# Attention with a gated output on one core: the opening stage recorded by the planner's clocked loop instead of a hand-written order

## The chip, the cores and the metric

The kernel runs on one core of a Trainium2 chip. The metric is the device time of one execution in microseconds (us). Three runs of the kernel before gave a median of 683.1 us (683.1 to 683.62).

## What is computed

```python
xn = layernorm(x)                       # x: 2048 tokens x 512
q = xn @ wq                             # 32 heads of 16
k = xn @ wk; v = xn @ wv                # one head of 16, shared by all
p = softmax(q k^T / 4)                  # 2048 x 2048 for each head
s = (p v) @ wo
g = silu(silu(xn @ w1) @ w2)            # 512 -> 1792 -> 512
out = x + s * g
```

## The kernel before

**Blocks.** The 32 heads by 2048 queries make 32 groups, each of four heads by 512 queries. A group runs over 16 key tiles of 128. One group and one key tile are a tile (512 in all), and one head of it is a block of 128 keys by 512 queries (2048 in all). TensorE computes a block's scores with one matmul (line 577). The exponential goes one of two ways. The first, called A, is ScalarE's exponential over two blocks at once, 128x1024, out of the two PSUM tiles psA (`exp_A`, line 606). The second, called D, is VectorE: `exp_D` (line 628) writes 16-bit integers whose bits are a rough exponential, and GpSimd adds two shifted copies of a whole tile (line 639). A tile of D thus has three versions, weighted to a better exponential, and costs three products with v where a tile of A costs one. D takes its scores from the banks D, D1 (the two halves of psD) and F (psF). The products with v gather in psO by fours (`emit_PV`, line 676). D's versions are kept in four slots: three of `ph_sb` and one made of the part of `x_sb` that holds the first 12 token tiles. A tile's slot is its running number modulo 4.

**The rest of the work.** The layer norm goes by quarters of 512 tokens, each of four token tiles. VectorE takes statistics (line 338) and aggregates them (341), GpSimd makes the reciprocal root by a power (345, 347), VectorE computes the bias -mean times rstd (359) and normalises (369). TensorE transposes (377), VectorE copies out (389), and TensorE and VectorE make k (412, 424) and v (438, 445). k is then copied by four small DMAs on SyncE's queue to a second layout for odd groups (430). Later there are dense jobs in bank F, called q, h, z and w (844), with a tanh on ScalarE for h and z (882).

**What sets the order.** `Sched` keeps a model clock for each engine and turns each recorded operation into an instruction with its semaphore waits. After the opening, one loop (from line 1111) asks the model when TensorE is free and when ScalarE needs its next scores, gives the time between to dense jobs and products with v in slots of 0.2163 us, and picks VectorE's next task among those that are ready (`advance_v`). The opening is not recorded by this loop. It is a list by hand: the first quarter (lines 467 to 489), then 12 key tiles of the first group, all on A (`NFRONT`, lines 1084 to 1108), with the layer norm's VectorE work at given tiles (`dve_pre`, 505), the TensorE work of the later quarters at given halves of tiles (`pe_pre`, 534), and matmuls on zeros (`warm`, 329) where there was nothing else. Banks are fixed there: transposes in psD, the halves of k in F and D1, v in D.

Of the kernel before, what the change touches and what calls it, by code (L numbers as in the profile page):

```python
# [13 lines left out]
P = 128  # L14
DH = 16
NQ = 512
# [180 lines left out]
def bass_recurrent_scan__grouped_kv_mqa__dense_activation_silu__prompt_kernel(  # L197
# [33 lines left out]
    AGE2 = 12.0  # L231
    KEEP, ENDQ, ROUND, MAXJOB, AHEAD, Q_EARLY = 0.6, 12, 3.0, 2, 3, 0.20
    LEAD, LEAD_END, SLIP, AGE, AGE1, MARGIN = 3, 3, 0.15, 2.0, 1.2, 0.0
    NF, F_FROM, F_LEFT, F_LATE, DENSE_END, HOLD, F_BEHIND = 14, 0.05, 9, 3, 0.95, 10, 0

    with ExitStack() as es:
# [32 lines left out]
        nb_sb = sb("nb_sb", [P, NT], FP32)  # L269
# [23 lines left out]
        def load_x(a, b, queue="sp"):  # L293
            op(queue, lambda e: e.dma_start(x_sb[:, a:b, :], xv[:, a:b, :]), writes=[("x", t) for t in range(a, b)],
               lane=f"lx{a}", cost=2.0 if b - a == 1 else 5.0)
# [5 lines left out]
        op("sp", lambda e: e.dma_start(wkn_sb[:], A_wk.rearrange("(dc p) e -> p dc e", p=P)), writes=["wkn"], lane="lwk")  # L301
        load_x(4, 8)
        op("sp", lambda e: e.dma_start(wq_sb[:], A_wq.rearrange("(dc p) n -> p dc n", p=P)), writes=["wq"], lane="lwq", cost=8.0)
        op("sp", lambda e: e.dma_start(wv_sb[:], A_wv.rearrange("(dc p) e -> p dc e", p=P)), writes=["wv"], lane="lwv")
# [6 lines left out]
        op("gp", lambda e: e.memset(mhalf_sb[:], -0.5), writes=["mhalf"])  # L311
        op("gp", lambda e: e.memset(scr_i[:], 0), writes=["scri"])
        op("v", lambda e: e.memset(zero_sb[:], 0.0), writes=["zero"])

# [22 lines left out]
        def stats(t):  # L337
            op("v", lambda e: e.bn_stats(stats_sb[:, t, :], x_sb[:, t, :]), reads=[("x", t)], writes=[("st", t)])  # L338

        def aggr(t):  # L340
            op("v", lambda e: e.bn_aggr(mv_sb[:, t, :], stats_sb[:, t, :]), reads=[("st", t)], writes=[("mv", t)])
# [8 lines left out]
        def rstd_sqrt(c):  # L350
            sl = slice(4 * c, 4 * c + 4)
            op("v", lambda e: e.tensor_scalar(rstd_sb[:, sl], mv_sb[:, sl, 1], LN_EPS, None, op0=ALU.add),
               reads=[("mv", t) for t in tiles(c)], writes=[("rstd", c)])
            op("a", lambda e: e.activation(rstd_sb[:, sl], rstd_sb[:, sl], ACT.Sqrt), reads=[("rstd", c)], writes=[("rstd", c)])
            op("v", lambda e: e.reciprocal(rstd_sb[:, sl], rstd_sb[:, sl]), reads=[("rstd", c)], writes=[("rstd", c)])

        def nbias(c):
            sl = slice(4 * c, 4 * c + 4)
            op("v", lambda e: e.scalar_tensor_tensor(out=nb_sb[:, sl], in0=mv_sb[:, sl, 0], scalar=-1.0, in1=rstd_sb[:, sl],
                                                     op0=ALU.mult, op1=ALU.mult),  # L360
               reads=[("mv", t) for t in tiles(c)] + [("rstd", c)], writes=[("nb", c)])

        def normalise(t, eng):
            rd = [("x", t), ("rstd", t // 4), ("nb", t // 4)]
            if eng == "a":
                op("a", lambda e: e.activation(xn_sb[:, t % 8, :], x_sb[:, t, :], ACT.Identity, bias=nb_sb[:, t:t + 1],
                                               scale=rstd_sb[:, t:t + 1]), reads=rd, writes=[("xn", t % 8)])
            else:
                op(eng, lambda e: e.tensor_scalar(xn_sb[:, t % 8, :], x_sb[:, t, :], rstd_sb[:, t:t + 1], nb_sb[:, t:t + 1],  # L369
                                                  op0=ALU.mult, op1=ALU.add), reads=rd, writes=[("xn", t % 8)])  # L370

        psT = psD[:, :].bitcast(BF16)

        def transposes(t):
            def f(e):
                for dc in range(NDC):
                    r = e.transpose(psT[:, (t % 4) * NQ + dc * P:(t % 4) * NQ + (dc + 1) * P], xn_sb[:, t % 8, dc * P:(dc + 1) * P],  # L377
                                    ident[:, :])
                return r
            op("pe", f, reads=[("xn", t % 8), "ident"], writes=["D1" if t % 4 > 1 else "D"])  # L380

        def evac_T(c, half, eng):
            src = psT[:, 2 * half * NQ:(2 * half + 2) * NQ].rearrange("p (t dc q) -> p t dc q", t=2, dc=NDC)
            dst = xnT_sb[:, :, c * NQ + 2 * half * P:c * NQ + (2 * half + 2) * P].rearrange("p dc (t q) -> p t dc q", t=2)
            rd, wr = ["D1" if half else "D"], [("xnT", c, half)]
            if eng == "a":
                op("a", lambda e: e.activation(dst, src, ACT.Copy), reads=rd, writes=wr)
            else:
                op("v", lambda e: e.tensor_copy(dst, src), reads=rd, writes=wr)

        def first_T(t, bank, key, eng):
# [7 lines left out]
            op("pe", f, reads=[("xn", t), "ident"], writes=[key])  # L399
# [9 lines left out]
        def mm_K(c, bank, key, a=0, b=NQ):  # L409
# [7 lines left out]
            op("pe", f, reads=rd + ["wkp"], writes=[key])  # L417

        def evac_K(c, bank, key, a, b, writes, eng="v"):
            dst, src, wr = kT_sb[0][:, c * NQ + a:c * NQ + b], bank[:, a:b], [("kT", 0, w) for w in writes]  # L420
            if eng == "a":
                op("a", lambda e: e.activation(dst, src, ACT.Copy), reads=[key], writes=wr)
            else:
                op("v", lambda e: e.tensor_copy(dst, src), reads=[key], writes=wr)  # L424
# [9 lines left out]
        def mm_V(c, bank, key):  # L434
# [6 lines left out]
            op("pe", f, reads=xnT_keys(c) + ["wv"], writes=[key])  # L441

        def evac_V(c, bank, key):
# [5 lines left out]
                reads=[key, "phw"], writes=[("v", c)])  # L449

        def mm_Q(c, t, dcs=range(NDC)):
            def f(e):
                for dc in dcs:
                    r = e.matmul(psF[:, :], lhsT=wq_sb[:, dc, t * P:(t + 1) * P], rhs=xnT_sb[:, dc, c * NQ:(c + 1) * NQ],
                                 start=(dc == 0), stop=(dc == NDC - 1))
                return r
            op("pe", f, reads=xnT_keys(c) + ["wq"], writes=["F"], cost=("full", [None] * len(dcs), NQ))

        def evac_Q(c, t, eng):
            dst = qT_sb[:, c % 2, t, :]  # L460
            if eng == "a":
                op("a", lambda e: e.activation(dst, psF[:, :], ACT.Copy, scale=QSCALE), reads=["F"], writes=[("qT", c % 2, t)])
            else:
                op("v", lambda e: e.tensor_scalar(dst, psF[:, :], QSCALE, None, op0=ALU.mult), reads=["F"], writes=[("qT", c % 2, t)],
                   cost=0.69)
# [7 lines left out]
        nbias(0)  # L473
        normalise(0, "v")
        normalise(1, "a")
        normalise(2, "v")
        normalise(3, "gp")
        first_T(0, psD[:, 0:NQ], "D", "a")
        first_T(1, psD[:, NQ:2 * NQ], "D1", "a")
        first_T(3, psA[0][:, 0:NQ], "A0", "v")  # L480
        first_T(2, psO[:, :], "O", "v")
        mm_K(0, psA[1], "A1", 0, P)
        evac_K(0, psA[1], "A1", 0, P, ["first"], "a")
        op("a", lambda e: e.activation(scr_sb[:, 0:1], rstd_sb[:, 0:1], ACT.Exp), reads=[("rstd", 0)], writes=["scr"])
        stats(4)
        warm(NWARM2, psF[:, :], "F")
        mm_Q(0, 0)
        mm_K(0, psO, "O", P, NQ)
        evac_Q(0, 0, "v")


        def ln_rest(c):
            nbias(c)
            for t in tiles(c):
                normalise(t, "v")

        def ln_aggr(c):
            for t in tiles(c):
                aggr(t)
            rstd_pow(c)  # L500

        def first_add():
            op("gp", lambda e: e.int64_add(scr_i[:, :].bitcast(I64), scr_i[:, :].bitcast(I64), 1), reads=["scri"], writes=["scri"])

        dve_pre = {
            0: [lambda: evac_K(0, psO, "O", P, NQ, [0, 1]), lambda: move_K(0), late_loads, lambda: stats(5), lambda: stats(6), lambda: stats(7),
                lambda: ln_aggr(1), lambda: evac_V(0, psD, "D"), lambda: stats(8), lambda: stats(9)],
            1: [lambda: ln_rest(1)],
            3: [lambda: stats(10), lambda: stats(11), lambda: ln_aggr(2)],
            4: [lambda: ln_rest(2)],  # L510
            5: [lambda: stats(12), lambda: stats(13)],
            7: [lambda: stats(14), lambda: stats(15), lambda: ln_aggr(3), first_add],
            8: [lambda: ln_rest(3)],
        }

        def quarter_T(c, t):
            transposes(4 * c + t)
            if t % 2:
                evac_T(c, t // 2, "v")

        def quarter_K(c):
            mm_K(c, psF, "F", 0, NQ // 2)

        def quarter_K2(c):
            mm_K(c, psD[:, NQ:2 * NQ], "D1", NQ // 2, NQ)
            evac_K(c, psF, "F", 0, NQ // 2, [2 * c])
            evac_K(c, psD[:, NQ:2 * NQ], "D1", NQ // 2, NQ, [2 * c + 1])
            move_K(c)

        def quarter_V(c):  # L530
            mm_V(c, psD, "D")
            evac_V(c, psD, "D")

        pe_pre = {}
        for c in (1, 2, 3):
            if c == 1:
                pe_pre[(1, 1)] = lambda: [quarter_T(1, 0), quarter_T(1, 1)]
                pe_pre[(2, 0)] = lambda: [quarter_T(1, 2), quarter_T(1, 3), quarter_K(1)]
            else:
# [259 lines left out]
        def next_job(t):  # L799
            if sum(h == "job" for h in hold.values()) >= MAXJOB:  # L800
                return None
# [422 lines left out]
```

## Time and profile before

| what | us |
|---|---|
| median of three runs | 683.1 |
| the profiled execution | 684.74 |
| its span (what the trace covers) | 682.9 |
| ScalarE busy | 665.0 (97%) |
| TensorE matmuls busy | 640.3 (94%) |
| VectorE busy | 589.6 (86%) |
| GpSimd busy | 369.3 (54%) |
| first exponential starts | 11.84 |
| first D copy-out starts | 37.88 |
| last exponential ends | 673.68 |

PE is TensorE, PEld its weight loads, DVE VectorE, ACT ScalarE, POOL GpSimd, SP SyncE. L606 is line 606. A row of the timeline gives start, duration, engine, line, operation, output, input, shapes, how many were merged, and in brackets the idle time before it with what ended it. The duration of a merged row runs from the first start to the last end. A row of the windows gives the stretch, then for each engine the busy time and the number of instructions, the granted TensorE clock as a share of full speed, and DMA.

### The profile page before, as it was taken

The page shows a single profiled execution, that of the slowest core. Times are in us where ns is not written, and L with a number is a line of the kernel's source. Part 1 is how long each engine was busy: PE and PEld are TensorE (multiplying, and loading weights), DVE is VectorE, ACT ScalarE, POOL GpSimd, SP SyncE. Part 2 cuts the span into 40 slices and gives each one's busy share as a digit, 9 for nine tenths or more (in the row PEclk, how much of TensorE's full clock was granted, in tenths as well). Part 3 has the DMA queues.
Part 4 walks back from the last instruction along what each step waited for, and adds up shares of the span by engine and source line. Part 5 has one row for each costly group of instructions (what it writes and reads, how often), then busy time and mean ns, then how long its engine had stood idle before and what let it go on. Part 6 is the DMA issues. An engine that isn't in the chain of part 4 may idle for free.

```text
span 682.9 us, 14794 instructions
## 1 busy us (share of the span) xinstructions
PE 640.3 (94%) x6224; PEld 185.9 (27%) x6303; DVE 589.6 (86%) x976; ACT 665.0 (97%) x759; POOL 369.3 (54%) x375
## 2 busy tenths in 40 slices
PE   8999999999999999999999999999999999999986
PEld 3432222222222222222222222222222222222222
DVE  7788888779898889988888898998898989889985
ACT  5999999999999999999999999999999999999995
POOL 5134554456565556465564565556555556756553
PEclk9999999999999999999999999999999999999999
DMA  8310000000000001000000000000000000000100
GB/s 296 119 36 1 1 2 1 1 1 2 1 1 1 2 16 32 16 3 1 1 1 2 2 1 1 17 17 16 18 1 1 1 1 2 1 2 16 48 1 32
DMA packets 10194, 12.25 MB, mean 18 GB/s; under 512 B 2000, under 2 KB 9424, under 8 KB 10128
## 3 DMA queue, kind: packets, MB, share of 16 engines
q1 hardware_dynamic: 8960, 7.25, 3.6%
q0 software_dynamic: 736, 3.67, 1.5%
q8 instruction: 49, 0.80, 0.5%
q10 hardware_dynamic: 432, 0.39, 0.2%
q14 instruction: 17, 0.14, 0.1%
HBM read 8.95 MB, written 2.10 MB: 16 GB/s over the span
## 4 chain that ended last, share of the span: by engine, by line
ACT 88%; PE 7%; DVE 3%; DMA 0%; POOL 0%; issue 0%; DVEq 0%
ACT pa_sb L606 83%; ACT t_sb L882 5%; PE psA L577 2%; PE psO L676 2%; DVE stats_sb L338 1%; PE psF L844 1%; PE psF L329 0%; DVE ph_sb L628 0%; DMA x_sb<-in_A_x_dram 0%; PE psD L377 0%; DVE xn_sb L369 0%; POOL rstd_sb L347 0%; PE psD L412 0%; PE psF L412 0%; DVE kTa_sb L424 0%
## 5 line engine op out<-in xcount | busy, mean ns | idle before, releaser
L606 ACT ACTIVATE pa_sb<-psA 128x1024 bf16<-128x1024 f32 x678 | 644.4, 1189 | 3.9 <-PE psA L577 2.0
L639 POOL INT64_ADD ph_sb<-ph_sb x260 | 268.7, 1046 | 214.6 <-DVE ph_sb L628 214.6
L628 DVE TENSOR_SCALAR ph_sb<-psD 128x512 int16<-128x512 f32 (+1 forms) x464 | 321.9, 703 | 49.8 <-PE psD L577 41.3
L676 PE MATMUL psO<-ph_sb,vaug_sb 128*32 128x512 bf16 x1560 | 204.0, 385 | 0.4 <-ACT pa_sb L606 0.2
L676 PE MATMUL psO<-pa_sb,vaug_sb 128*32 128x512 bf16 x1356 | 202.9, 385 | 0.6 <-DVE vaug_sb L445 0.3
L577 PE MATMUL psA<-qT_sb,kTa_sb 32*128 32x512 bf16 x692 | 134.2, 384 | 10.2 <-ACT pa_sb L606 7.0
L577 PE MATMUL psA<-qT_sb,kTb_sb 32*128 32x512 bf16 x664 | 129.2, 386 | 11.8 <-ACT pa_sb L606 9.8
L639 POOL INT64_ADD x_sb<-x_sb x86 | 89.0, 1047 | 63.1 <-DVE x_sb L628 63.1
L577 PE MATMUL psD<-qT_sb,kTb_sb 32*128 32x512 bf16 x327 | 120.1, 386 | 0.4 <-DVE ph_sb L628 0.4
L628 DVE TENSOR_SCALAR x_sb<-psD 128x512 int16<-128x512 f32 (+1 forms) x149 | 104.0, 702 | 15.2 <-PE psD L577 14.0
L577 PE MATMUL psD<-qT_sb,kTa_sb 32*128 32x512 bf16 x309 | 112.0, 384 | 0.0
L676 PE MATMUL psO<-x_sb,vaug_sb 128*32 128x512 bf16 x516 | 92.9, 386 | 0.1
L577 PEld LDWEIGHTS psA<-qT_sb,kTa_sb 32*128 32x128 bf16 x692 | 32.5, 91 | 141.8 <-ACT pa_sb L606 129.0
L577 PEld LDWEIGHTS psA<-qT_sb,kTb_sb 32*128 32x128 bf16 x664 | 31.2, 91 | 144.5 <-ACT pa_sb L606 132.9
L676 PEld LDWEIGHTS psO<-ph_sb,vaug_sb 128*32 128x32 bf16 x1560 | 51.7, 95 | 50.7 <-issue 33.1
L844 PE MATMUL psF<-xnT_sb,w_sb 128*128 128x512 bf16 x194 | 60.9, 384 | 3.9 <-issue 2.4
L844 PE MATMUL psF<-w_sb,u_sb 128*128 128x512 bf16 x205 | 61.3, 383 | 2.5 <-issue 1.9
L676 PEld LDWEIGHTS psO<-pa_sb,vaug_sb 128*32 128x32 bf16 x1356 | 50.8, 94 | 45.2 <-issue 30.1
L882 ACT ACTIVATE t_sb<-psF 128x512 bf16<-128x512 f32 x72 | 55.2, 766 | 0.0
L914 DVE SCALAR_TENSOR_TENSOR u_sb<-t_sb,psF 128x512 bf16<-128x512 bf16 x56 | 38.3, 683 | 8.3 <-ACT t_sb L882 7.8
L577 PEld LDWEIGHTS psD<-qT_sb,kTb_sb 32*128 32x128 bf16 x327 | 28.3, 91 | 0.9 <-DVE ph_sb L628 0.7
L676 PEld LDWEIGHTS psO<-x_sb,vaug_sb 128*32 128x32 bf16 x516 | 23.1, 95 | 16.0 <-issue 11.2
(98 smaller groups left out, 361.1 us busy)
## 6 DMA issues: line engine op xcount, KB each, us to landing
w_sb<-in_B_w_dram POOLq DMA_DIRECT2D x2, 1792.0 KB, 12.3
x_sb<-in_A_x_dram SPq DMA_DIRECT2D x18, 128.0 KB, 2.3
out_dram<-ob_sb SPq DMA_DIRECT2D x15, 128.0 KB, 1.7
x_sb<-in_A_x_dram SPq DMA_DIRECT2D x3, 512.0 KB, 6.9
wq_sb<-in_A_wq_dram SPq DMA_DIRECT2D x1, 512.0 KB, 6.4
wop_sb<-in_A_wo_dram SPq DMA_DIRECT2D x1, 512.0 KB, 10.1
x_sb<-in_A_x_dram ACTq DMA_DIRECT2D x2, 128.0 KB, 3.1
kTb_sb<-kTa_sb SPq DMA_DIRECT2D x16, 16.0 KB, 2.9
```

The lines of the kernel that those rows point to most:

```text
L338: op("v", lambda e: e.bn_stats(stats_sb[:, t, :], x_sb[:, t, :]), reads=[("x", t)], writes=[("st", t)])
L577: return e.matmul(ap, lhsT=kT_sb[g % 2][32 * i:32 * i + 32, kt * P:(kt + 1) * P], rhs=qT_sb[32 * i:32 * i + 32, c % 2, g // 2, :], start=T ...
L606: d = op("a", lambda e: e.activation(pa_sb[:, sl, :], psA[k][:, :], ACT.Exp, scale=ESCALE), reads=["A%d" % k], writes=[("pa", sl)], cost=2 ...
L628: d = op("v", lambda e: e.tensor_scalar(ph_ap(0, sl, 512 * pos, 512 * pos + m), src, float(PH_ONE + PH_BIAS), 0.0, op0=ALU.add, op1=ALU.ma ...
L639: d = op("gp", lambda e, j=j: e.int64_add(ph_ap(j, sl, 0, 2048).bitcast(I64), ph_ap(0, sl, 0, 2048).bitcast(I64), PH_SHIFT[j] * 0x00010001 ...
L676: r = e.matmul(psO[32 * i:32 * i + 32, :], lhsT=vaug_sb[:, p["v"], p["kt"], :], rhs=p["ap"], start=s0, stop=s1, tile_position=(0, 32 * i), ...
L844: h = e.matmul(ap, lhsT=l, rhs=r, start=(m == 0), stop=(m == end))
L882: op("a", lambda e: e.activation(t_sb[:, n % 2, :], bank_ap(b), ACT.Tanh, scale=0.5 if jb[0] == "h" else 0.25), reads=[b], writes=[("t", n ...
L914: op("v", lambda e: e.scalar_tensor_tensor(out=dst, in0=t_sb[:, n % 2, :], scalar=1.0, in1=src, op0=ALU.add, op1=ALU.mult), reads=tk["read ...
```

## The change

The order of the opening after the first quarter comes from the loop. Statistics, aggregation, normalisation and copies out become VectorE tasks with ranks (`st`, `ag`, `nm`, `T`, `K`, `V`). Transposes, k and v of the later quarters become front jobs, which the loop puts in whichever of D, D1 and F is free. The lists by hand and their zero matmuls go; the loop's own filler stays.

The first quarter changes too. All four first normalisations are on VectorE, as subtract the mean and multiply by rstd, so the bias instruction goes in all quarters. The root is taken by ScalarE directly from the variance with a bias of eps, and the Exp table is asked for right after it. q's first 128 columns are computed in two halves of 256 tokens, each copied out by ScalarE. Three of the second quarter's statistics stand ahead of this. The loads of wo, w1 and w2 are recorded after the second quarter's power on GpSimd's queue.

For D, a tile's slot is chosen when the tile is opened (`free_slot`), not by its running number. While k isn't complete, only one tile of the second group may go to D, and none of the first. GpSimd's shifted copies are held back until its last power has been recorded. SLIP goes from 0.15 to 0.2.

```diff
-    AGE2 = 12.0
+    AGE2, AGE_ST, FIRST, FRONT_D, FRONT_K, SHORT, ST_EARLY, Q_ACT = 12.0, 1.5, 9.4, 1, 4, 0, 3, 1
-    LEAD, LEAD_END, SLIP, AGE, AGE1, MARGIN = 3, 3, 0.15, 2.0, 1.2, 0.0
+    LEAD, LEAD_END, SLIP, AGE, AGE1, MARGIN = 3, 3, 0.2, 2.0, 1.2, 0.0
...
         def rstd_sqrt(c):
             sl = slice(4 * c, 4 * c + 4)
-            op("v", lambda e: e.tensor_scalar(rstd_sb[:, sl], mv_sb[:, sl, 1], LN_EPS, None, op0=ALU.add),
-               reads=[("mv", t) for t in tiles(c)], writes=[("rstd", c)])
-            op("a", lambda e: e.activation(rstd_sb[:, sl], rstd_sb[:, sl], ACT.Sqrt), reads=[("rstd", c)], writes=[("rstd", c)])
-            op("v", lambda e: e.reciprocal(rstd_sb[:, sl], rstd_sb[:, sl]), reads=[("rstd", c)], writes=[("rstd", c)])
+            op("a", lambda e: e.activation(rstd_sb[:, sl], mv_sb[:, sl, 1], ACT.Sqrt, bias=eps_sb[:, 0:1]),
+               reads=[("mv", t) for t in tiles(c)] + ["eps"], writes=[("rstd", c)], cost=4)
+            op("a", lambda e: e.activation(scr_sb[:, 0:1], mhalf_sb[:, 0:1], ACT.Exp), reads=["mhalf"], writes=["scr"], cost=4)
+            K.act_end += 1.28
+            op("v", lambda e: e.reciprocal(rstd_sb[:, sl], rstd_sb[:, sl]), reads=[("rstd", c)], writes=[("rstd", c)], cost=0.2)
...
         def normalise(t, eng):
+            op(eng, lambda e: e.tensor_scalar(xn_sb[:, t % 8, :], x_sb[:, t, :], mv_sb[:, t, 0:1], rstd_sb[:, t:t + 1],
+                                              op0=ALU.subtract, op1=ALU.mult),
+               reads=[("x", t), ("mv", t), ("rstd", t // 4)], writes=[("xn", t % 8)], cost=0.41)
...
-        nbias(0)
-        normalise(0, "v")
-        normalise(1, "a")
-        normalise(2, "v")
-        normalise(3, "gp")
+        for t in tiles(0):
+            normalise(t, "v")
         first_T(0, psD[:, 0:NQ], "D", "a")
         first_T(1, psD[:, NQ:2 * NQ], "D1", "a")
+        first_T(2, psO[:, :], "O", "v")
         first_T(3, psA[0][:, 0:NQ], "A0", "v")
-        first_T(2, psO[:, :], "O", "v")
         mm_K(0, psA[1], "A1", 0, P)
         evac_K(0, psA[1], "A1", 0, P, ["first"], "a")
-        op("a", lambda e: e.activation(scr_sb[:, 0:1], rstd_sb[:, 0:1], ACT.Exp), reads=[("rstd", 0)], writes=["scr"])
-        stats(4)
+        for t in range(4, 4 + ST_EARLY):
+            stats(t)
         warm(NWARM2, psF[:, :], "F")
-        mm_Q(0, 0)
+        first_Q((0, 1), psF, "F")
+        first_Q((2, 3), psD, "D")
+        first_evac_Q(0, 2, psF, "F", "a")
+        first_evac_Q(2, 4, psD, "D", "a" if Q_ACT else "v")
+        for t in range(4 + ST_EARLY, 8):
+            stats(t)
+        for t in range(4, 8):
+            aggr(t)
+        rstd_pow(1)
         mm_K(0, psO, "O", P, NQ)
-        evac_Q(0, 0, "v")
+        evac_K(0, psO, "O", P, NQ, [0, 1])
+        move_K(0)
+        late_loads()
...
+        RANK = dict(T=0, K=0, V=0, ag=2, nm=3, st=4)
...
+        for c in range(1, NC):
+            if c > 1:
+                for t in tiles(c):
+                    task("st", ln_st, 0.687, t=t, reads=[("x", t)], writes=[])
+                task("ag", ln_ag, 0.4, c=c, reads=[], writes=[], need=[("st", t) for t in tiles(c)])
+            for t in tiles(c):
+                task("nm", ln_nm, 0.41, t=t, reads=[("rstd", c)], writes=[], need=[("ag", c)] + ([("T", t - 8)] if t >= 8 else []))
...
+        front = [("V", 0)] + [jb for c in range(1, NC) for jb in (("T", c, 0), ("T", c, 1), ("K", c, 0), ("K", c, 1), ("V", c))]
...
+        def next_front(t):
+            return next((jb for jb in front[:2] if front_ready(jb, t)), None)
...
         def next_job(t):
+            if progress() < F0:
+                return None
...
+        def free_slot(gi):
+
+            used = {slot_of[o["idx"]] for o in dst["open"] + dst["fifo"]}
+            best = None
+            for sl in range(NPD):
+                if sl in used or (sl == 3 and not all(("nm", n) in tok for n in range(12))):
+                    continue
+                keys = {ph_key(j, sl, p) for j in range(NPH) for p in range(4)}
+                n = [sum(p["key"] in keys for p in q) for q in pend]
+                if any(n[gi + 1:]) or any(slot_of[a[1]] == sl for a in shifts):
+                    continue
+                if best is None or sum(n) < best[0]:
+                    best = (sum(n), sl)
+            return None if best is None else best[1]
...
         def next_D(t):
...
+                    if ("kT", 0, NKT // 2 - 1) not in tok and (gi == 0 or NKT - len(left[gi]) >= FRONT_D or ("kT", 0, FRONT_K) not in tok):
+                        continue
+                    if free_slot(gi) is None:
+                        continue
...
         def fill_D(t, free):
...
+            if front:
+                keep = max(keep, len(banks) - 1 + sum(h == "blk" for h in hold.values()))
...
-        for u in range(NFRONT):
-            for _ in range(2):
-                exp_A(*front.pop(0))
-            for f in dve_pre.get(u, []):
-                f()
...
+        K.act_end = max(K.act_end, FIRST)
+        K.free["a"] = max(K.free["a"], FIRST - 0.3)
...
+            late = more and ast["tile"] is None and not kt_ready((group_A(), left[group_A()][0]), t + (0.1 if state["n"] else 0.4))
+            blocked = blocked or late
...
+                jb = next_front(t)
+                if jb and slots >= 2:
+                    b = free_banks(t + 0.04)
+                    if b:
+                        emit_front(jb, b[0])
+                        did = 2
+                can = job_ready(t) and not did
```

`front_ready` asks the model whether a job's inputs are there; `emit_front` records its matmuls in the bank and makes the copy-out a VectorE task; `first_Q` is four matmuls of 128 columns for each token tile; `kt_ready` asks whether a key tile's k has arrived.

## Prediction

> **What bounds the kernel now.** I read the page's busy line and its costliest group first, then ScalarE's timeline from the start, the chain of waits of the opening, VectorE's timeline there, and the stretches with a granted clock under 1.
>
> ```profile
> PE 640.3 (94%) x6224; PEld 185.9 (27%) x6303; DVE 589.6 (86%) x976; ACT 665.0 (97%) x759; POOL 369.3 (54%) x375
> L606 ACT ACTIVATE pa_sb<-psA 128x1024 bf16<-128x1024 f32 x678 | 644.4, 1189 | 3.9 <-PE psA L577 2.0
> ```
>
> ScalarE is the bound. A ledger shows how closely. The chain has 24 exponentials in 22.00 us, so 0.917 us each; 72 tanh add 0.49 us each. From the first start, 677 x 0.917 = 620.8, plus the last one's 1.02, plus 72 x 0.49 = 35.3, is 657.1 us. The first exponential starts at 11.84 and the last ends at 673.68, which is 661.8 us. So ScalarE loses only 4.7 us in all. Where?
>
> ```profile
> 9.42 1.28 ACT L484 ACT_TABLE_LOAD   x1
> 10.71 0.21 ACT L484 ACTIVATE scr_sb<-rstd_sb 128x1 bf16<-128x1 f32 x1
> 11.84 2.85 ACT L606 ACTIVATE pa_sb<-psA 128x1024 bf16<-128x1024 f32 x3 [0.92 <-PE psA L577]
> 15.07 3.98 ACT L606 ACTIVATE pa_sb<-psA 128x1024 bf16<-128x1024 f32 x4 [0.37 <-PE psA L577]
> 19.38 4.01 ACT L606 ACTIVATE pa_sb<-psA 128x1024 bf16<-128x1024 f32 x4 [0.33 <-PE psA L577]
> 37.84 14.81 ACT L606 ACTIVATE pa_sb<-psA 128x1024 bf16<-128x1024 f32 x16
> ```
>
> The last row is the 26th exponential, found by narrowing the window. At 0.917 us it would start at 11.84 + 25 x 0.917 = 34.77; it starts at 37.84. **The opening loses 3.07 us**, all on TensorE. The chain shows how:
>
> ```profile
> 15.88 0.54 PE psF L329 x2
> 16.42 0.33 PE psO L676 x4
> 16.75 0.32 PE psA L577 x2
> 17.07 0.55 PE psD L377 x8
> ```
>
> Two zero matmuls, one round of products and one pair of scores take 0.54 + 0.33 + 0.32 = 1.19 us where 0.917 is to be had. A half of a quarter's transposes with scores is 0.55 + 0.32 = 0.87, which fits.
>
> The other loss is late. In 656.00 to 659.00 TensorE is about half busy; then the clock is halved:
>
> ```profile
> 658.00:659.00 1.00, 0.47 (x6) 0.15 (x3) 1.00 (x4) 1.00 (x2) 1.00 (x2) 1.00 0.00 0
> 660.00:661.00 1.00, 1.00 (x10) 0.10 (x2) 1.00 (x3) 1.00 (x2) 0.44 (x1) 0.50 0.00 0
> 662.00:663.00 1.00, 1.00 (x12) 0.25 (x12) 0.00 (x0) 0.51 (x2) 0.71 (x1) 0.50 0.00 0
> ```
>
> (The clock is the third number from the end.) Exponentials starting at 660.08, 661.45, 662.97 and 664.29 span 4.21 us instead of 2.75: 1.46 us. 3.07 + 1.46 is 4.5 of the 4.7.
>
> Between these ScalarE is full, so there the time falls only if D takes tiles from A. D begins here:
>
> ```profile
> 31.60 0.17 DVE L359 SCALAR_TENSOR_TENSOR nb_sb<-mv_sb,rstd_sb 128x4 f32<-128x4 f32 x1 [1.17 <-POOL rstd_sb L347]
> 34.98 0.69 DVE L389 COPY xnT_sb<-psD 128x1024 bf16<-128x1024 bf16 x1 [0.94 <-PE psD L377]
> 37.88 0.69 DVE L628 TENSOR_SCALAR ph_sb<-psD 128x512 int16<-128x512 f32 x1 [0.26 <-PE psD L577]
> ```
>
> VectorE waits for GpSimd's power and for TensorE's transposes, and D starts when the layer norm is through, at 37.88. ScalarE does 678 x 2 = 1356 of 2048 blocks, 2.05 per us over 661.8 us. D does the other 692 until about 665, 1.10 per us.
>
> **The first quarter.** From the aggregates' end (6.25) before has 0.17 (line 352), the root, the reciprocal and 0.16 (line 359). The two that go cost 0.17 + 0.16 and two gaps of 0.03: 0.39 us. The normalisations start at 6.74 instead of 7.13, and on VectorE alone take 0.32 to 0.42 each (four in 1.38 at line 369), ends at 7.15, 7.47, 7.79, 8.11. But the gain is covered: the table load now stands between the root (6.29 to 6.49) and the first copies out. 6.51 + 1.28 + 0.21 = 8.00, and before the first copy started at 8.04. So ScalarE's copies (1.08 for two) and k's (0.28) end at 9.36 instead of 9.40: worth 0.04.
>
> The 1.28 + 0.21 at 9.42 go, but they lay beside q's matmuls and copy. The path there is TensorE's zero matmuls until 9.52 (same in both), then q. Now each token tile is 4 matmuls of 128 columns, 0.22 us as the transposes at 8.40. Two tiles end at 9.52 + 0.44 + 0.19 (the drain: 1.04 for four of 512 against 4 x 0.213) = 10.15, the next two at 10.59. ScalarE's copy of 256 columns is bounded by its 0.28 for 128 and 1.02 for 1024; interpolated it is 0.39. The second ends at 11.02, against VectorE's 11.27 before. k's remaining matmuls (0.65) end at 11.05, beside it. With 0.03 to 0.14 to the scores and 0.43 to the exponential as before, the first starts at **11.5** (11.3 by 0.28, 11.9 if the copy costs the 0.69 of VectorE's and they queue). Worth 0.3 us. wq lands at 2.66 + 6.4 = 9.06, in time by 0.46.
>
> The Trainium skill's page "ScalarE: Activation LUTs", section "What ACT_TABLE_LOAD costs", speaks against this place for the load: it gives a switch about 2.66 us, with a drain. By it, the first copy would start 1.38 us later. The trace has 1.28 us, with the copy of k ending at 9.40 and the next instruction at 10.71, so no drain shows here. By the page's figure the saving below would be 0.9 us less (1.38 x 0.65).
>
> **Key tiles in time.** Exponentials 1 to 8 need the first quarter's k; the second quarter's must be there at 11.5 + 8 x 0.917 = 18.8, less 0.43. VectorE has three statistics after 9.03 and a fourth (0.62 each), then aggregates until 11.9, so GpSimd's power (0.24 + 1.04) ends at 13.3, not 15.35. Normalisation, transposes, copy, half of k and its copy took 15.39 to 19.55 before, 4.2 us: 17.5, in time by 0.9. The later quarters have more.
>
> **Loads and GpSimd.** w1 and w2 move from 8.07 to about 13.3 on GpSimd's queue, behind the power. They took 12.3 us and land by 29; the first tanh was at 52.45. Nothing. Ahead of GpSimd's first shifted copy lie 5.9 us of idle "issue" before line 503; it now starts when the last power ends, some 5 us earlier, and four slots cover it.
>
> **Front jobs.** 16 jobs take 0.5 to 0.6 us of TensorE each, one in a gap of scores, and products only where two more slots remain. Bounds of what ScalarE still loses: 0 and the 3.07 of before. I take 0.8, nearer to the row in which 0.87 fits into 0.917, with some products colliding. Worth 2.3.
>
> **D's start.** VectorE was busy 18.9 us from 11.84 to 36.00 and 0.8 more until 37.88: 19.7. Three biases go (0.5), two statistics move ahead (1.2): 18.0 from 11.5, so 29.5 at best. Before it idled 6.3; I leave 1.5, since statistics can now fill waits: **D from 31.0**, 6.9 us earlier. Bounds: 29.5 and 37.9.
>
> **The sum.** ScalarE is ahead by 0.3 + 2.3 = 2.6 us, D by 6.9. If the end comes s earlier, the blocks gained and given up at the end balance: 2.05 (2.6 - s) + 1.10 (6.9 - s) = 0, s = (5.3 + 7.6) / 3.15 = 4.1 us. That is about three more blocks on D, nearly one tile. The profiled execution's span 682.9 becomes 678.8 (its time 684.74 becomes 680.6; 1.6 of that lies over the median). The median 683.1 becomes **679.0**.
>
> Free slots and SLIP are charged at nothing: products and banks decide D's rate now (VectorE idles 41.3 us waiting for scores in ph_sb's rows). One tile of D more or less is two exponentials, 1.83 us.
>
> **Rivals.**
> - D's head start is lost again at the end (lead and group ends are unchanged): only 2.6 us remain, 680.5. For it: tiles come whole, and 2.8 us of net lead times 1.10 is only three blocks.
> - The clock drop at 660 doesn't recur: up to 1.46 us more, 677.6. For it: it followed one stretch at half load, and the order changes. Two tiles more on D instead: 2.6 + 3.66, 676.8.
> - The front jobs wait as before, or the clock drops in the opening, where 11 recorded zero matmuls go: one drop costs 1.46. ScalarE keeps 0.3 us and D two blocks: 682.3. Against it: filler stays, and TensorE's useful work is denser. The skill's page "TensorE: Matmul & The Clock Gate" ("What's actually happening") says that low activity over a window of about 3.4 us halves the clock; the drop at 660 agrees, after 3 us at 0.47 to 0.56 busy.
> - **Slower**: `free_slot` refuses tiles in the steady part, since a slot that owes products to a later group is shut at opening, where before only the copy-out waited. Each refused tile is 1.83 us. Beyond two it eats the 4.1; with four of 173, 683.1 - 4.1 + 7.3 = 686.3. Against it: any of four slots may now serve.
> - The order isn't what it claims (a misjudged landing stalls one queue): also under the last two.
>
> **The numbers.** Forecast 0.36; lead lost 0.20; no clock drop or more tiles 0.24; opening no better 0.10; slower 0.10. 0.2% (1.4 us) is about what a measurement here can tell from no change: faster means under 681.7. The first three cases and a little of the fourth are faster, 0.82; same 0.09; slower 0.09. The range takes in the first four: 675.5 (more tiles and no drop) to 683.0.
>
> **What would show it.** The first exponential at 11.5; the 26th by 35.3; the first steady D copy-outs near 31; some 676 exponentials; the table load at 6.5 with the first copy at 8.0. A first exponential after 12, gaps <-PE psA in the opening, or over 680 exponentials would prove me wrong.

## The result and the profile after

The changed kernel takes 687.81 us (median of 8 runs, 686.95 to 689.76). The kernel before, run beside it, takes 683.37 us (683.1 to 686.04). The ratio is 1.0061, with a 95% interval of 1.0042 to 1.008: 4.4 us slower by the medians, where 4.1 us faster was forecast. (A run that took over 1.5% longer than its kernel's fastest, one of e5's twelve and two of e8's below, is left out of the ratios but not of the medians.) The profiled execution has a span of 686.4 us (time 688.22), 3.5 us more than before.

The page of the changed kernel, busy line and costliest group:

```profile
PE 640.7 (93%) x6232; PEld 186.9 (27%) x6310; DVE 591.9 (86%) x985; ACT 664.3 (97%) x760; POOL 368.9 (54%) x373
L547 ACT ACTIVATE pa_sb<-psA 128x1024 bf16<-128x1024 f32 x678 | 642.8, 1177 | 7.2 <-PE psA L518 6.2
```

The work is the same: 678 exponentials, as before. What grew is the last figure, the idle time ahead of the exponentials: 7.2 us instead of 3.9, of which 6.2 instead of 2.0 wait for A's scores (line 518). ScalarE's timeline of the changed kernel says where they lie:

```profile
6.62 1.28 ACT L355 ACT_TABLE_LOAD   x1
8.02 1.07 ACT L392 ACTIVATE xnT_sb<-psD 128x512 bf16<-128x512 bf16 x2
10.81 0.38 ACT L454 ACTIVATE qT_sb<-psF 128x256 bf16<-128x256 f32 x1 [1.44 <-PE psF L446]
12.23 11.10 ACT L547 ACTIVATE pa_sb<-psA 128x1024 bf16<-128x1024 f32 x12 [0.56 <-PE psA L518]
23.60 3.77 ACT L547 ACTIVATE pa_sb<-psA 128x1024 bf16<-128x1024 f32 x4 [0.27 <-PE psA L518]
31.23 1.02 ACT L547 ACTIVATE pa_sb<-psA 128x1024 bf16<-128x1024 f32 x1 [3.86 <-PE psA L518]
33.17 2.11 ACT L547 ACTIVATE pa_sb<-psA 128x1024 bf16<-128x1024 f32 x2 [0.92 <-PE psA L518]
35.65 17.52 ACT L547 ACTIVATE pa_sb<-psA 128x1024 bf16<-128x1024 f32 x19 [0.37 <-PE psA L518]
```

The table load stands where the prediction put it, and the first copy starts at 8.02. The 13th exponential is at 23.60, the 20th at 35.65. Seven at 0.917 us are 6.42; they take 12.05. So **5.6 us are lost between 23.6 and 35.7**, mostly in three gaps. The 26th starts at 41.09; before it was 37.84. That is 3.25 later, and the span is 3.5 longer: nearly all of the difference between the two profiles arises before this point.

The chain of waits of the changed kernel (start, duration, what) names the cause:

```profile
18.57 10.91 DMA kTb_sb<-kTa_sb
29.52 0.60 PE psD L518
30.12 0.53 PE psF L428 x16
30.66 0.54 PE psA L518 x2
```

A small DMA lies on it: the copy of the second quarter's k to the layout for odd groups (16 KB each, line 420), issued at 18.57 and landed at 29.5. TensorE's timeline shows who waits:

```profile
25.77 0.39 PE L518 MATMUL psA<-qT_sb,kTa_sb 32*128 32x512 bf16 x2
29.52 0.60 PE L518 MATMUL psD<-qT_sb,kTb_sb 32*128 32x512 bf16 x1 [3.36 <-DMA kTb_sb<-kTa_sb]
30.06 0.60 PE L428 MATMUL psF<-wv_sb,xnT_sb 128*128 128x16 bf16 x16
30.59 0.61 PE L518 MATMUL psA<-qT_sb,kTa_sb 32*128 32x512 bf16 x2
```

This is the one early D tile that the change allows (FRONT_D = 1). It belongs to the second group, which is odd and reads kTb. Its first score stands in TensorE's queue at 26.15 and waits 3.36 us. The next scores for ScalarE, ready to run, stand behind it. After the wait the matmuls take 0.60 us instead of 0.39. The windows of the changed kernel (stretch, length, busy time of PE, PEld, DVE, ACT, POOL, granted clock, DMA share, GB/s) show why:

```profile
24.00:28.00 4.00, 2.16 (x17) 0.90 (x14) 2.64 (x5) 3.37 (x4) 0.00 (x0) 1.00 0.93 302
28.00:32.00 4.00, 2.48 (x31) 1.00 (x31) 1.28 (x6) 0.77 (x1) 0.42 (x2) 0.50 0.09 24
```

The clock is halved from 28 us on, still in the wait, until about 34. And the DMA engines are nearly full until 28: w1 and w2 (3.67 MB) now go out at 13.30 and 14.46 on GpSimd's queue, not at 8.07 and 9.14. wo (512 KB) is on SyncE's own queue, in both kernels; here it goes out at 14.99, just ahead of the copy, and lands 14.0 us later, at 29.0: half a microsecond before it.

So the theory after the result was: a late copy of k, read too early, holds TensorE, and the clock drop adds to it. Its rivals: the wait is only where another loss shows; the clock drop is the greater part; and, for the copy itself, full engines against a queue of its own that is blocked.

### The profile page after: what moved, and what is told of

Read it like the earlier page. It is cut to its first block, busy times and chain, and to the rows that moved or that the text cites. A ratio compares the mean times of both kernels' runs of the same rounds, so it can differ in the third digit from the quotient of the medians.

```text
span 686.4 us, 14802 instructions
## 1 busy us (share of the span) xinstructions
PE 640.7 (93%) x6232; PEld 186.9 (27%) x6310; DVE 591.9 (86%) x985; ACT 664.3 (97%) x760; POOL 368.9 (54%) x373
## 3 DMA queue, kind: packets, MB, share of 16 engines
q0 software_dynamic: 736, 3.67, 1.5%
## 4 chain that ended last, share of the span: by engine, by line
ACT 89%; PE 6%; DMA 3%; DVE 1%; issue 0%; SPq 0%; DVEq 0%
ACT pa_sb L547 84%; ACT t_sb L914 5%; PE psO L629 2%; PE psA L518 2%; DMA kTb_sb<-kTa_sb 2%; DMA wq_sb<-in_A_wq_dram 1%; PE psF L876 1%; PE psF L330 0%; PE psD L518 0%; DVE ph_sb L569 0%; SPq L294 0%; DVE x_sb L569 0%; PE psA L1201 0%; DVE wq_sb L1214 0%; DVE onb_sb L712 0%
## 5 line engine op out<-in xcount | busy, mean ns | idle before, releaser
L589 POOL INT64_ADD ph_sb<-ph_sb x294 | 304.3, 1048 | 233.8 <-DVE ph_sb L569 233.6
L569 DVE TENSOR_SCALAR ph_sb<-psD 128x512 int16<-128x512 f32 (+1 forms) x528 | 359.8, 691 | 54.9 <-PE psD L518 43.9
L629 PE MATMUL psO<-ph_sb,vaug_sb 128*32 128x512 bf16 x1764 | 212.9, 385 | 0.3 <-POOL ph_sb L589 0.2
L518 PE MATMUL psA<-qT_sb,kTa_sb 32*128 32x512 bf16 x692 | 134.8, 386 | 10.1 <-ACT pa_sb L547 6.9
L518 PE MATMUL psD<-qT_sb,kTa_sb 32*128 32x512 bf16 x309 | 113.4, 384 | 0.4 <-DVE ph_sb L569 0.4
L589 POOL INT64_ADD x_sb<-x_sb x52 | 53.8, 1046 | 44.6 <-DVE x_sb L569 44.6
L569 DVE TENSOR_SCALAR x_sb<-psD 128x512 int16<-128x512 f32 (+1 forms) x95 | 65.9, 699 | 12.0 <-PE psD L518 10.3
L629 PEld LDWEIGHTS psO<-ph_sb,vaug_sb 128*32 128x32 bf16 x1764 | 53.4, 95 | 56.0 <-issue 37.8
L629 PE MATMUL psO<-x_sb,vaug_sb 128*32 128x512 bf16 x312 | 54.5, 384 | 0.0
L569 DVE TENSOR_SCALAR ph_sb<-psF 128x512 int16<-128x512 f32 x51 | 34.5, 676 | 0.0
```

The costliest lines, as they stand in the source:

```text
L518: return e.matmul(ap, lhsT=kT_sb[g % 2][32 * i:32 * i + 32, kt * P:(kt + 1) * P], rhs=qT_sb[32 * i:32 * i + 32, c % 2, g // 2, :], start=T ...
L569: d = op("v", lambda e: e.tensor_scalar(ph_ap(0, sl, 512 * pos, 512 * pos + m), src, float(PH_ONE + PH_BIAS), 0.0, op0=ALU.add, op1=ALU.ma ...
L589: d = op("gp", lambda e, j=j: e.int64_add(ph_ap(j, sl, 0, 2048).bitcast(I64), ph_ap(0, sl, 0, 2048).bitcast(I64), PH_SHIFT[j] * 0x00010001 ...
L629: r = e.matmul(psO[32 * i:32 * i + 32, :], lhsT=vaug_sb[:, p["v"], p["kt"], :], rhs=p["ap"], start=s0, stop=s1, tile_position=(0, 32 * i), ...
```

## The experiments

Each kernel is the changed kernel with the edit shown. "Before" is always run on the same chip.

### Who waits: e1 and e3

```diff
-    ... = 12.0, 1.5, 9.4, 1, 4, 0, 3, 1
+    ... = 12.0, 1.5, 9.4, 0, 4, 0, 3, 1     (e1: FRONT_D = 0)
```

> The changed kernel, but no tile of the second group may go to D before all of k is there (FRONT_D 0). In the changed kernel's trace TensorE stands still from 26.15 to 29.52 at the early D tile's first scores, which read a copy of k whose DMA was issued at 18.57 and landed 10.9 us later, and the clock is 0.50 afterwards; ScalarE loses 5.6 us between 23.60 and 35.65. Theory W (this wait): the gap of 3.86 us and the halved clock go, the 26th exponential starts near 36, and the time is 682.5 to 684.5. Rival S (free_slot and SLIP make D slower in the steady part): the opening mends but the time stays over 686. Rival L (the moved loads hurt in more ways than this wait): some gap over 2 us remains in the opening, 685 to 687.

Measured: 681.79 us, ratio 0.9962 (0.9946 to 0.9979). The copy is as slow as ever (up to 11.0 us), but no one reads it early. ScalarE's timeline of e1 has 26 exponentials in a row:

```profile
23.40 23.94 ACT L547 ACTIVATE pa_sb<-psA 128x1024 bf16<-128x1024 f32 x26 [0.27 <-PE psA L518]
```

In e3 the early D tile stays, but the planner's model takes the copy for 12 us long, and so takes a key tile of the first quarter for it:

```diff
-                   writes=[...], lane=f"mk{c}{i}")
+                   writes=[...], lane=f"mk{c}{i}", cost=12.0 if c == 1 else 3.0)
```

> The changed kernel with one number of the model changed: the copy of the second quarter's k is charged 12 us instead of 3. TensorE's order stays the same by name; the early D tile takes a key tile of the first quarter, whose copy was issued at 12.5. Theory W: the wait at 26.15 goes or falls under 1 us, 682 to 684.5. If the wait were for the bank or the queue and not for this copy, nothing changes: 687.5 to 688.

Measured: 681.94 us, 0.9967 (0.9954 to 0.9981). The D score runs at 25.54 without a wait, and 26 exponentials start from 23.36 without a gap. The early tile does no harm; its reading of the late copy does. Both undo the loss and leave a gain over before.

### Which load makes the copy late: e2, e7, e13, e14

e2 issues w1 and w2 early again (8.54 and 9.62); e7 issues them late (22.02 and 23.10), behind the third quarter's power and the landing of the second quarter's copies.

```diff
 def late_loads():
     wo on SyncE's queue
-    w1, w2 on GpSimd's queue
...
 (e2: right behind the four first normalisations)
+    w1, w2 on GpSimd's queue, reads=[("xn", 3)]
 (e7: in ln_ag, behind the third quarter's power)
+    w1, w2 on GpSimd's queue, reads=[("kT", 1, 2, i) for i in range(4)]
```

> The changed kernel, with the loads of w1 and w2 recorded before the second quarter's power, behind the fourth normalisation, so that GpSimd issues them near 8.3 as the kernel before did. Theory W with the moved loads as its cause: the second quarter's copy of k, issued near 18.6, lands within 6 us, the early D tile's scores do not wait or by under 0.5 us, and the time is 682 to 684.5. Rival: if the copy is slow whatever else runs, the wait stays and so does 687 to 688. Rival S: the wait goes and the time stays over 686.

> The changed kernel with w1 and w2 loaded still later, behind the third quarter's power on GpSimd and behind the landing of the second quarter's copy of k. It tests that the copy was slow because of these loads. If so: the copy issued near 18.5 lands in 3 to 4 us as the first quarter's did (2.7 median at 12.5), the early D tile does not wait, and the time is 680.5 to 682.5. If small copies between the two layouts are slow by themselves, it lands 8 us or more after issue, and the time is 684 to 688.

Measured: e2 682.47 us, 0.9973 (0.9959 to 0.9987); e7 683.43 us, 0.9986 (0.9973 to 0.9999). In e2 the wait is all but gone, yet the copy still takes 8 us, as its chain and TensorE's timeline show:

```profile
18.03 7.97 DMA kTb_sb<-kTa_sb
```

```profile
26.05 0.39 PE L518 MATMUL psD<-qT_sb,kTb_sb 32*128 32x512 bf16 x1 [0.44 <-DMA kTb_sb<-kTa_sb]
```

In e7 w1 and w2 have not yet started: the second quarter's copies land in 1.8 to 2.5 us, and wo, still ahead of them, in 4.3. But the loads now meet the later quarters' copies, and the loss only moves to the last one. The chain of e7, and its ScalarE:

```profile
34.43 4.41 DMA kTb_sb<-kTa_sb
```

```profile
40.75 2.12 ACT L545 ACTIVATE pa_sb<-psA 128x1024 bf16<-128x1024 f32 x2 [2.10 <-PE psD L516]
```

So w1 and w2 matter, but e2 did not fit "full engines" alone: in e2 wo lands at 25.8 and the copy at 26.0, in the changed kernel at 29.0 and 29.5. wo stands ahead of the copy in its own queue. e13 and e14 move wo and nothing else; w1 and w2 stay at 13 to 14, and the order on TensorE, VectorE and ScalarE is the changed kernel's.

```diff
 def late_loads():
-    wo on SyncE's queue
     w1, w2 on GpSimd's queue
+    wo on GpSimd's queue                       (e14)
...
 def move_K(c):
     four copies of k on SyncE's queue
+    if c == 1: wo on SyncE's queue             (e13)
```

> One load moved: wo's 512 KB on SyncE's queue goes from before the second quarter's copies of k to behind them; w1 and w2 stay where the change put them (GpSimd, issued at 13.3 and 14.5). The order on every engine is otherwise that of the changed kernel. Theory 1 (the copy's own queue): in the changed kernel wo lands at 29.0 and the copy of k at 29.5, in e2 25.9 and 26.0; the copy is 10.9 us late because 512 KB stand ahead of it in its own queue, and these move slowly beside w1 and w2. Then the copy now lands within 4 us of its issue at 18.6 (before 23), the score of the early D tile at 26.1 does not wait, the 13th to 20th exponentials have no gap, and the time is that of e1 and e3, 681.5 to 682.5. Theory 2 (the engines are full, whatever the queue): the copy still lands 8 to 11 us after its issue, TensorE still waits some 3 us at 26.1, and the time stays at 687 to 688.

> wo's load leaves SyncE's queue altogether and stands behind w1 and w2 on GpSimd's; the order on the other engines is the changed kernel's. The same total of bytes moves in the same stretch. Theory 1 (own queue): the copy of k lands within 4 us of its issue, no wait at 26.1, 681.5 to 682.5. Theory 2 (full engines): the copy is as late as before, 8 to 11 us, and the time stays at 687 to 688. If w1 and w2 hold back everything on SyncE's queue only while w1 moves (to about 20.4 in the changed kernel), the copy lands at 20.5 to 21.5.

Measured: e13 682.07 us, 0.996 (0.9947 to 0.9973); e14 681.93 us, 0.9962 (0.995 to 0.9974). TensorE and ScalarE of e13:

```profile
25.68 0.39 PE L519 MATMUL psD<-qT_sb,kTb_sb 32*128 32x512 bf16 x1
```

```profile
23.50 24.16 ACT L548 ACTIVATE pa_sb<-psA 128x1024 bf16<-128x1024 f32 x26 [0.27 <-PE psA L519]
```

**Moving one 512 KB load behind the copy gives back the whole loss.** But the first theory's "within 4 us" missed: the copies take 6.0 to 6.5 us in e13 and 6.8 to 7.0 in e14, and the first of them is in time by 0.7 (18.5 + 6.5 = 25.0 against 25.68). The time of the copy adds up: about 2 us before w1 and w2 start (e7, wo ahead of it), 6.5 beside w1 and w2 (e13), 10.9 behind wo as well. Each theory had a part. It takes both loads to make the copy 3.4 us late: with wo out of the way (e13) it is in time, and with w1 and w2 early (e2) it is late by 0.44.

How slowly wo moves is seen in the DMA view of the changed kernel from 21 to 27 us (queue: packets, MB, share of 16 engines). q0 is GpSimd's queue (its 3.67 MB in all are w1 and w2), q1 is SyncE's:

```profile
q0 software_dynamic: 404, 1.66, 80.0%
q1 hardware_dynamic: 406, 0.42, 23.1%
```

The two queues move packet for packet. w2's packets are 4 KB (1.66 MB by 404), wo's 1 KB, so SyncE's queue gets a fifth of the bytes: 0.42 MB in 6 us.

### The wait or the clock: e6, e9, e10

e6 and e9 keep the wait but put 14 matmuls on zeros ahead of the waiting score, so that TensorE does not idle. e6 charged the planner's model a short matmul for them, e9 nothing. e10 is the changed kernel, unedited, beside e9.

```diff
+def cold():
+    14 matmuls of zero_sb, 128x512, into bank F        cost: ("full", [], 0) in e9
...
+    if o["idx"] == 0 and pos == 0:
+        cold()
```

> The changed kernel with 14 zero matmuls (3.0 us) on TensorE's queue ahead of the early D tile's first scores, so that they fill the wait from 26.15 to 29.52; the model is charged one short matmul for them. It separates the wait from the halved clock. In the changed kernel ScalarE loses 3.9 us in the wait and another 1.7 us until 35.65, while TensorE's clock is 0.50. If that 1.7 comes from the clock: the clock stays 1.00 through 28 to 34, the gap of some 3.9 us stays, and the time is near 686 (1 to 2 less than 687.8). If TensorE has room enough at half its clock: 687.5 to 688.

> As the sixth run, 14 zero matmuls ahead of the early D tile's first scores, but charged nothing in the model, so that the order of all other instructions is that of the changed kernel (the sixth run's order differed and ended with 682 exponentials instead of 678, so its time did not answer). If the halved clock costs time: the clock stays 1.00 from 28 to 34, only the wait's 3 to 4 us are lost in the opening instead of 5.6, and the time is 1.5 to 2.5 us under that of the changed kernel in the next run. If it costs nothing: the same time within 0.5 us.

> The changed kernel again, unchanged, as the partner of the run before on the same chip: 687 to 688.5, the wait of over 3 us at the early D tile's scores and the clock at 0.50 behind it.

Measured: e6 689.48 us, 1.0077 (1.0054 to 1.01); e9 686.56 us, 1.0034 (1.0018 to 1.005); e10 688.18 us, 1.0091 (1.0059 to 1.0124). e6 decides nothing: the small charge shifted the planner's later choices to 171 D tiles and 682 exponentials, 4 x 0.917 = 3.7 us more for ScalarE. In e9 the order is the changed kernel's. The windows of e9, and then of e10:

```profile
30.00:32.00 2.00, 2.00 (x24) 0.60 (x23) 1.26 (x6) 1.64 (x2) 1.15 (x2) 1.00 0.03 8
```

```profile
30.00:32.00 2.00, 2.00 (x27) 0.90 (x30) 1.22 (x6) 0.67 (x1) 0.33 (x2) 0.50 0.04 8
```

The clock (third from the end) is whole in e9 and halved in e10. From the 13th exponential to the 20th, e10 loses 6.05 us; e9 loses 3.8, nearly all in one gap:

```profile
30.30 15.07 ACT L547 ACTIVATE pa_sb<-psA 128x1024 bf16<-128x1024 f32 x16 [3.58 <-PE psA L518]
```

By the medians the halved clock is worth 688.18 - 686.56 = 1.6 us, or 1.25 against the 687.81 of the first measurement. The rest of the way to e1 is some 5 us; the trace of e9 shows 3.8 of it as the wait in the opening, and where the last microsecond goes isn't shown. The rival "mostly the clock" falls; it is about a quarter.

### What D's early start is worth, and the best version: e4, e11, e12, e15, e16

e4 joins e1 and e2; e12 is e4 again, run later beside e9 to e11. e11 is e4 with one D tile of the first, even group allowed early. e15 is e2 with wo behind the copies as in e13 (early D tile kept); e16 is e4 with wo there.

```diff
 (e11)
-    ... and (gi == 0 or NKT - len(left[gi]) >= FRONT_D or ("kT", 0, FRONT_K) not in tok):
+    ... and (gi > 0 or dst["idx"] >= 0 or ("kT", 0, 2) not in tok):
```

> No early D tile and the loads of w1 and w2 early, both. Theory W: no more than either alone, 682 to 684.5, since each takes away the same wait. Rival L (the moved loads cost something besides): faster than the first of these runs by over 1 us. Rival S: over 686.

> The fourth run's kernel again (no early D tile, w1 and w2 early) as the partner of the run before on the same chip: 681 to 682.5, first exponential 2.1 us after wq lands or at 11.1 if wq lands before 9.

> No early tile of the second group, w1 and w2 early, and instead one tile of the first group to D as soon as the second quarter's first half of k is there; the first group reads k where TensorE's copy-out puts it and needs no DMA. In this order D has 174 tiles and ScalarE 676 exponentials, against 173 and 678 in the changed kernel, the kernel before and all other runs but the sixth. If an earlier D start is worth time only when a whole tile is won: 0.5 to 1.8 us under the next run. If the tile's VectorE work (4 x 0.69 us) holds up the layer norm instead: a gap in the opening and no gain.

> The early loads of e2 (w1 and w2 issued near 8.3) and wo behind the second quarter's copies; the early D tile is kept. Theory 1: the copy issued near 18 lands by 22, the 0.44 us wait of e2 at 26.05 and its 0.47 of ScalarE go; about 682.0, ratio 0.996 to 0.997. Theory 2: the copy still takes 8 us, the wait stays, 682.5.

> e4 (early loads, no early D tile) with wo behind the second quarter's copies. Nobody waits for the copy in e4, so both theories give e4's time, ratio 0.996, unless the copy of the second quarter is what delays D's steady start (33.9 in e4): then D starts up to 1 us earlier and the time falls by 0.3 us, which this measurement can't tell. It is run as the candidate for the best version and for the latency of the copy.

| kernel | us | ratio (95%) | D copy-outs by 45 us |
|---|---|---|---|
| before | 683.4 to 684.5 | 1 | 8 |
| e1 | 681.79 | 0.9962 (0.9946 to 0.9979) | 11 |
| e4 | 681.58 | 0.9963 (0.9947 to 0.9978) | 12 |
| e12 | 682.03 | 0.9964 (0.9948 to 0.9979) | 12 |
| e13 | 682.07 | 0.996 (0.9947 to 0.9973) | 15 |
| e15 | 681.26 | 0.996 (0.9947 to 0.9974) | 16 |
| e16 | 682.3 | 0.9962 (0.9947 to 0.9977) | 12 |
| e11 | 682.43 | 0.9966 (0.9954 to 0.9979) | 15 |

All are some 2.5 us faster than before, and none can be told from another. D's start differs by a whole tile (four copy-outs) between e1 and e13, at no difference in time. e13's first steady copy-out is close to the forecast 31.0 (VectorE's timeline; the early tile's is at 27.39):

```profile
30.24 0.68 DVE L570 TENSOR_SCALAR ph_sb<-psD 128x512 int16<-128x512 f32 x1
```

Yet e1, e4, e12, e13, e15 and e16 all have 678 exponentials, like before. D's lead never became a tile. It could not on the chip: the planner fixes the number of tiles when it records the order, by its model clock, and e13's order on VectorE and ScalarE is the changed kernel's. e11 does get one more (676 exponentials, 174 tiles), and pays for it in the opening, as its ScalarE shows:

```profile
25.91 7.68 ACT L547 ACTIVATE pa_sb<-psA 128x1024 bf16<-128x1024 f32 x8 [0.89 <-PE psA L518]
34.47 12.98 ACT L547 ACTIVATE pa_sb<-psA 128x1024 bf16<-128x1024 f32 x14 [0.88 <-PE psD L518]
```

0.89 + 0.88 is 1.77 us lost against 2 x 0.917 = 1.83 won. e15 has the lowest median, but e13, the smallest edit, is as good as the measurement can tell.

### The load of wq: e5 and e8

e5 is e4 with wq's load issued ahead of the second quarter's x. e8 is e1 with that and e7's late loads, meant as the best of all.

```diff
-load_x(4, 8)
 wq on SyncE's queue
+load_x(4, 8)
```

> No early D tile and early w1 and w2 as in the run before this one, and wq's load issued ahead of the second quarter's x on SyncE's queue. In the four runs so far q's matmuls wait for wq, which lands at 9.6 to 10.1, and the first exponential starts 2.1 us later, at 11.7 to 12.2. If wq sets the first exponential: wq lands near 8.5 to 9, q starts behind the zero matmuls at 9.5, the first exponential starts at 11.3 to 11.5 and the time falls by 0.2 to 0.5 us against that run (681.6), to 681.1 to 681.4. Rival: the second quarter's x, now later, holds up VectorE's statistics and so the second quarter's k; a gap in ScalarE near 19 and no gain.

> No early D tile, w1 and w2 late as in the run before, wq first: nothing in the opening should wait for a DMA. The first exponential at 11.3 to 11.5, no gap over 0.6 us in the opening, 680.5 to 681.5. If late w1 and w2 hold up the first dense jobs (46 to 48), a gap or a later first tanh shows and it is no better than the fifth run.

Measured: e5 682.38 us, 0.9966 (0.9952 to 0.9981); e8 683.67 us, 0.9993 (0.997 to 1.0015). wq now lands 5.0 and 5.6 us after its issue, and the first exponential starts at 11.01 and 10.99. But e5 gains nothing over e4 that can be measured (0.45 us are lost again before 22.8), and e8 misses: it carries e7's fault (a copy of 4.64 us at 34.42, a gap of 1.00 at 40.39) and VectorE waits 0.6 us for the second quarter's x.

## Why the prediction was wrong

**The step that failed is "Loads and GpSimd".** It said that w1 and w2 "land by 29; the first tanh was at 52.45. Nothing." It asked only who reads w1 and w2. It did not ask what other transfers run between 15 and 29, though the copies of k do; these copies are in none of its sums. (Its 12.3 us is the median of the two loads; w2 alone took 15.2 and landed at 29.6.) It also did not price the wait that the change adds: one D tile of the second group, whose scores read that copy. The copy is due at 26.15 and lands at 29.5. What is queued behind the waiting score on TensorE is every score for ScalarE. The runs put 3.36 us of wait on TensorE, 3.86 on ScalarE, and with the slower clock 5.6 us in all. The bare sum: without this, 2.4 us faster (e13); with it, 4.4 slower.

That moving wo alone is enough (e13, e14) does not follow from full DMA engines. The profile had the sign: wo took 10.1 us from issue to landing before and takes 14.0 now, and SyncE issues it between the first and the second quarter's copies in both kernels. In the kernel before, the second quarter's copy, issued at 20.38, landed 4.2 us later, right behind wo. No one read it before 37.4, so it cost nothing there.

The other steps, one by one:

- **The first quarter.** Root, table load, first copies: 8.02 against the forecast 8.00, and ScalarE's copy of 256 columns 0.38 against 0.39. The first exponential was put at 11.5 and came at 12.23. The term that failed is wq, "in time by 0.46": it landed 7.45 us after its issue, not 6.4, as the chain of the changed kernel has it:

```profile
2.66 7.45 DMA wq_sb<-in_A_wq_dram
10.15 0.62 PE psF L446 x8
```

  With the same order of loads it took 5.7 to 7.3 us in the other profiles, and in those of the changed kernel's variants the first exponential came between 11.1 and 12.1. A margin of 0.46 was within that spread.
- **The table load.** No drain shows: the root starts at 6.31, the load at 6.62, the Exp at 7.92. The 2.66 us of the Trainium skill's page "ScalarE: Activation LUTs", section "What ACT_TABLE_LOAD costs", is not seen in this place either: the load takes 1.28 us, and the Exp starts 1.30 us after the load's start.
- **Key tiles in time.** Right: the first half of the second quarter's k was copied out by 17.6 (forecast 17.5), the power ended at 13.3 as forecast.
- **Front jobs.** 0.8 us of remaining loss was forecast. In e1 the 26th exponential starts at 35.23, where 12.03 + 25 x 0.917 = 34.95 would be without loss: 0.3. Right, and better than forecast.
- **D's start.** Right where the copy is in time: 30.24 in e13, forecast 31.0.
- **The sum.** Wrong in its second half. For e13 the formula gives (2.05 x 2.2 + 1.10 x 6.4) / 3.15 = 3.7 us, with 37.84 - 35.63 = 2.2 for ScalarE's 26th exponential and seven copy-outs more by 45 us, 7 / 1.10 = 6.4, for D. The runs give 2.4 (684.48 to 682.07): ScalarE's lead alone, within the measurement. The formula let the engines share out blocks at the end, but their number on each engine is fixed when the order is recorded, and D's lead, 7.6 / 3.15 = 2.4 us of the forecast, was worth nothing that can be measured. The rival "D's head start is lost again" (680.5, 2.6 faster) is what the cured kernels do, for the reason it gave: tiles come whole. That its 2.6 is so near is in part luck: e13's first exponential came 0.3 us later than before, not 0.3 earlier, and the rest of its opening gained 2.5.
- **The slower rival.** Wrong mechanism: D lost no tile, 678 exponentials and 173 D tiles are as before. The cause was in the list ("a misjudged landing stalls one queue"), but without a place or a price.
- **The clock drop in the opening.** Named, at 1.46 us; it came, by the wait and not by the missing zero matmuls (the clock falls at 28.0, 1.9 us after TensorE goes idle at 26.15), and cost 1.25 to 1.6.

What stays open: why the copies need 6.5 us and not 2 beside w1 and w2 when nothing of their own queue is ahead of them. The last section shows that part of it passes before their packets start to move; what holds them no run here took apart.

## What to carry to other kernels

When a load is moved, ask not only who reads it, but which small transfers will stand behind it in its queue and which will run beside it, and compare their new landing with the time at which each is read. A speculative piece of work on an in-order engine must be sure of its input, since a wait there holds everything behind it; here the cure was one load placed behind the small copies. And a lead on the engine that is not the bound is worth nothing until it becomes a whole unit of moved work.

## What the hardware showed that was not expected

- **Two queues with bulk loads under way share the engines packet for packet, not byte for byte** (404 against 406 packets, 1.66 against 0.42 MB). The Trainium skill's page "DMA: Bandwidth & Descriptors", section "Queues, rings and completion order", says that an engine takes turns between the queues, a packet at a time; the counts agree. Small copies that come while GpSimd's queue already fills the engines don't get such a turn at once. In the kernel before, from 12 to 15 us, with four of SyncE's copies of k issued from 11.81 on, the DMA view has GpSimd's queue alone, with w1's packets of 7 KB:

```profile
q0 software_dynamic: 171, 1.23, 100.5%
```

  Those copies landed 5.4 to 6.2 us after their issue. In e13, from 20.5 to 22.5 us, with the second quarter's copies issued from 18.47 on, it is alone again, now with 4 KB a packet in the mean, mostly w2's:

```profile
q0 software_dynamic: 174, 0.70, 100.8%
```

- **The late clock drop is a matter of the execution.** e4 and e12 are the same kernel, with spans of 679.6 and 682.0. e4's profile has no drop at 660 and ends on an unbroken run of exponentials; e12's has it, with gaps such as 0.50 us ahead of 662.16. So 1 to 2 us of a single profile's span may be chance, and the comparison of runs decides.
